# Cosine phases by an integer quarter turn on GpSimd, logs stacked on 64 rows, and another order of the round list

## The chip, the cores and the metric

The kernel runs on one core of a Trainium2 chip, in one launch. A core has five engines with queues of their own: TensorE (PE in the profile, with its weight loads as PEld), VectorE (DVE), ScalarE (ACT), GpSimd (POOL) and SyncE (SP, which only issues DMAs here). Each works its own queue in order and waits for semaphores. The metric is the device time in microseconds.

## The reference, cut to what matters

The block has two halves with a layer norm ahead of each, modulated by six vectors that a small product makes from `c`. The first half is a state space model (S4): a convolution along the 2048 positions, separately for each of 640 channels, with a kernel that is a sum over 128 complex exponentials.

```python
logdA = dt * (A_re + 1j * A_im)              # 640 x 128
dB = dt * (B_re + 1j * B_im)
P = jnp.exp(logdA[:, :, None] * l[None, None, :])      # l = 0 .. 2047
K = jnp.einsum("dn,dnl,dn->dl", Cc, P, dB).real        # 640 x 2048
y = irfft(rfft(u) * rfft(K)) + u * Dskip               # padded to 4096
x = x + ga * y
```

The second half is a gated product: `x + gb * ((silu(h w1) * (h w3)) w2)` with 640 x 1728 weights. The change touches the first half only.

## The kernel before, in words

The 2048 positions are split in 32 times 64. The exponential of the complex log at position 64 a + b is written as a magnitude times a cosine or sine of a phase, in a slow table (over a, 32 entries) and two fast ones (over b). The kernel K is then a small product over the 128 states, and both the convolution's transforms are products with constant matrices.

**Preparation.** `polar` (L237) takes the parameters of a slice of channels and makes magnitude logs and phases: the log of the magnitude per position (`are * dtc`), the log of the factor C times B, and the phases as integers, where 2^32 is a whole turn (`thi` for the turn per position, `phi` for the starting phase). It runs for channels 0 to 127 first with VectorE doing most products (`polar(d0, V)`), and for the other 512 in three stages in the loop over the first steps, with GpSimd in VectorE's place at some lines. Its last stage writes each log into `lt` in another order of columns, has TensorE transpose it into PSUM (L283), and splits it into a rounded part (`lah`, `lmh`, a copy on ScalarE) and the remainder (`lal`, `lml`, a subtraction on VectorE). TensorE's fast float mode keeps too few digits of one operand for a log; the two parts together have them.

**Steps.** The 640 channels are worked in 40 steps (`NS`) of 16 channels (`SD`). The names of the parts of a step s, as they stand in the round list:

- `PH`: `phases`, on GpSimd. L472 multiplies `thi` by the integers of `iota` (128x1024 integers, which wrap around at a turn) and L473 adds `phi` to the first 32 columns of each channel (128x512). The tile `ph` has four buffers.
- `AB`: `absph`, `CO`: `cosine`, `SI`: `sine`, all on ScalarE. The absolute value of the phase goes to the tile `cs` (three buffers), and the cosine is the sine of a quarter turn less that value, with the bias tile `hp`. The sine is taken of the phase in place.
- `PA`, `XA`, `PQ`, `XQ`: TensorE multiplies the logs by position tables (`exp_fast`, L432; `exp_slow`, L444), each for two ranges of 32 of the 128 contraction rows, and for rounded part and remainder as instructions of their own. ScalarE takes the exponential out of PSUM into the table `A`. Both products of all steps use one PSUM buffer (tag B) in the rounds.
- `E1`, `E2`, `A1`, `A2`: `real1` (L497, 128x1024), `real2` (L500, 128x512), `imag1` (L504, 128x1024), `imag2` (L508, 128x512) on VectorE: magnitudes times cosines into `E` (two buffers), magnitudes times sines in place in `A`. All their operands lie in SBUF.
- `kg` (L521), `K` (L528, L529), `pt` (L539), `uk`: the small product on TensorE, its scaling on VectorE, a first transform on TensorE, and a copy on ScalarE.

Ten steps behind, the convolution works on pieces k: `st` (L570, TensorE), `kc` (a copy on ScalarE), `T` (L587, L588: two products on VectorE, one operand in PSUM), `Y` (L594, L595: a difference and a sum, one operand in PSUM), `iv` (L612, TensorE) and `zt` (a copy on ScalarE and the store by SyncE). The PSUM buffer of `st` is single up to piece 38, so that `st` of k + 1 waits for `Y` of k.

**Order.** Steps 0 to 9 go through a loop over `tk`, beside the layer norm and a first transform of its result, with the order within an engine left to the framework but for ScalarE, whose order is the program's. From step 10 on the order is written out by hand: `ROUND` (L826) is a list of words, each a part and an offset, played once for every four steps (`EB`), and every instruction keeps its place in the queue of its engine. A part that has been done, or that is out of range, is passed over. A last loop (L846) does what is left of the convolution. Then the gated product begins.

Of the kernel before, what the change touches and what calls it, by code (L numbers as in the profile page):

```python
# [9 lines left out]
F32 = mybir.dt.float32  # L10
F32R = mybir.dt.float32r
I32 = mybir.dt.int32
# [5 lines left out]
P = 128  # L18
L = 2048
D = 640  # L20
# [87 lines left out]
def tile_kernel(ctx: ExitStack, tc: tile.TileContext, a):  # L108
# [28 lines left out]
    def acopy(out, in_):  # L137
        return tc.keep_in_program_order(S.copy(out, in_))  # L138
# [17 lines left out]
    gaT = kp.tile([P, D // 4], F32, name="gaT")  # L156
    dz = kp.tile([P, D // 4], F32, name="dz")
    V.memset(dz, 0.0)
    hp = kp.tile([P, 1], F32, name="hp")
    V.memset(hp, math.pi / 2)  # L160
    sc = kp.tile([P, KD], F32, name="sc")
    cT = kp.tile([P, KD], F32, name="cT")
    uk = kp.tile([P, 3, NA, DC], F32, name="uk")
# [6 lines left out]
    once = lambda shape, dt, name: tp.tile(shape, dt, name=name, bufs=1)  # L170
    thi = once([P, D], I32, "thi")
    phi = once([P, D], I32, "phi")
    lah = once([P, KD, P], F32R, "lah")
    lal = once([P, KD, P], F32R, "lal")
    lmh = once([P, KD, P], F32R, "lmh")
    lml = once([P, KD, P], F32R, "lml")
    r2 = once([P, NA, NB], F32R, "r2")
    r1 = once([P, NA, NA], F32R, "r1")
    sel = once([P, NA], F32R, "sel")
# [15 lines left out]
    flat = [uk[:, i].rearrange("p f d -> p (f d)") for i in range(3)]  # L195
    prm = flat[0][:, :6 * D].rearrange("p (i d) -> p i d", i=6)
    ldt, dt, m0, t3, gr, gi = (flat[2][:, i * D:(i + 1) * D] for i in range(6))

    def w_load(w, c0):

# [36 lines left out]
    def polar(cs, E):  # L237

        are, aim, br, bi, cr, ci = (prm[:, i, cs] for i in range(6))
        ld, dtc, m, t, g_r, g_i = (v[:, cs] for v in (ldt, dt, m0, t3, gr, gi))  # L240
        k0, nk = cs.start // P, (cs.stop - cs.start) // P

        E.tensor_tensor(g_r, br, cr, op=OP.mult)
        E.tensor_tensor(m, bi, ci, op=OP.mult)
        E.tensor_tensor(g_r, g_r, m, op=OP.subtract)
        V.tensor_tensor(g_i, br, ci, op=OP.mult)
        V.tensor_tensor(t, bi, cr, op=OP.mult)
        V.tensor_tensor(g_i, g_i, t, op=OP.add)
# [24 lines left out]

        nat = lambda v: v.rearrange("n (k p r j) -> n k r p j", k=nk, p=4, r=4)
        rows = lambda v: v[:, :nk * P].rearrange("n (k r p j) -> n k r p j", k=nk, p=4, r=4)
        for k in range(nk):
            E.tensor_tensor(rows(lt[:, 0])[:, k], nat(are)[:, k], nat(dtc)[:, k], op=OP.mult)
        for k in range(nk):
            V.tensor_tensor(rows(lt[:, 1])[:, k], nat(q)[:, k], nat(ld)[:, k], op=OP.add)
        for i, (hi, lo) in enumerate(((lah, lal), (lmh, lml))):  # L280
            pT = psS.tile([P, 2, 512], F32, name="pT", tag="AB"[i], bufs=1)
            for k in range(nk):
                PE.transpose(pT[:, 0, k * P:(k + 1) * P], lt[:, i, k * P:(k + 1) * P], ident)  # L283
# [132 lines left out]
    ph, cs, AA, EC, PK, K1 = {}, {}, {}, {}, {}, {}  # L416

    def exp_rows(s):
        return s // SPC, slice((s % SPC) // 2 * 8, (s % SPC) // 2 * 8 + 8), [
            (rr, slice((2 * (s % 2) + rr) * 32, (2 * (s % 2) + rr) * 32 + 32)) for rr in range(2)]  # L420

    pA, pQ = {}, {}

    def exp_fast(steps):

        for s in steps:
            pA[s] = psS.tile([P, 2, 512], F32, name="pa", tag="AB"[s % 2] if not in_order[0] else "B", bufs=1)
        for w, st in ((lah, True), (lal, False)):
            for s in steps:
                ch, js, rows = exp_rows(s)  # L430
                for rr, r in rows:
                    keep(PE.matmul(pA[s][:, rr, :], w[r, ch, :], r2[r, js, :].rearrange("p j b -> p (j b)"),  # L432
                                   start=st, stop=not st, tile_position=(r.start, 0)))

    def exp_slow(steps):

        for s in steps:
            pQ[s] = psS.tile([P, 2, 512], F32, name="pq", tag="AB"[s % 2] if not in_order[0] else "B", bufs=1)
        for i, (w, rt) in enumerate(((lah, r1), (lal, r1), (lmh, None), (lml, None))):
            for s in steps:  # L440
                ch, js, rows = exp_rows(s)
                for rr, r in rows:
                    rv = bc(sel[r, js], 2, NA) if rt is None else rt[r, js, :]
                    keep(PE.matmul(pQ[s][:, rr, :256], w[r, ch, :], rv,  # L444
                                   start=(i == 0), stop=(i == 3), tile_position=(r.start, 0)))

    def fast(s):

# [25 lines left out]
        ph[s] = p  # L474

    def absph(s):
        c = tp.tile([P, SD, NPH], F32, name="cs", bufs=3)
        act(c, ph[s], AF.Abs)
        cs[s] = c

    def cosine(s):
        act(cs[s], cs[s], AF.Sin, scale=-2 * math.pi / TURN, bias=hp)

    def sine(s):
        sn = ph[s].bitcast(F32)
# [11 lines left out]
        keep(V.tensor_tensor(EC[s][:, :, 1:3, :], AA[s][:, :, 1:3, :], mid(cs[s]), op=OP.mult))  # L497

    def real2(s):
        keep(V.tensor_tensor(EC[s][:, :, 0, :], AA[s][:, :, 0, :], cs.pop(s)[:, :, 2 * NA - 1:NA - 1:-1], op=OP.mult))  # L500

    def imag1(s):
        A = AA[s]
# [1 line left out]

    def imag2(s):
        A = AA[s]
        keep(V.scalar_tensor_tensor(A[:, :, 0, :], ph.pop(s)[:, :, 2 * NA - 1:NA - 1:-1], -1.0, A[:, :, 0, :],  # L508
                                    op0=OP.mult, op1=OP.mult))

    def tables(s):
# [262 lines left out]
    for tk in range(LAG):  # L774
# [49 lines left out]


    ROUND = (  # L826
# [5 lines left out]
    ).split()  # L832
    in_order[0] = True
    for rnd in range(NS // EB):
        for word in ROUND:
            name, k = word[:2].rstrip("+-"), EB * rnd + int(word[len(word[:2].rstrip("+-")):])
            do(name, k)
            if name == "E1" and 24 <= k < 32 and k % 2 == 0:
                x_load((k - 24) // 2)

            if name == "kg" and 36 <= k < 40:
# [681 lines left out]
```

## Time and profile before

| | |
|---|---|
| time, median of three runs | 984.4 us (982.26 to 985.58) |
| span of the profiled execution | 984.1 us, 20582 instructions |
| busy over the span: TensorE, VectorE, ScalarE, GpSimd | 918.2, 700.8, 541.1, 265.3 us |
| mean granted TensorE clock | 0.947 |
| HBM traffic | 142 GB/s over the span |

No time of the profiled execution other than its span is given, so sums are made against the span, which is 0.3 us under the median.

The span has four stretches: preparation (up to about 47 us), the loop over steps 0 to 9 (to about 173 us), the rounds and their end (to about 420 us), and the gated product. The shares over the whole span mix these; so the stages are read one by one, by the busy time of each engine in a window. A row of a group of instructions gives line, engine, operation, the tiles and their shapes and the count, then the busy time and the mean duration of one, then the idle time of the engine just before them and who ended it. A row in order of time begins with start and duration in us. Times of instructions that follow each other on one engine overlap by about a tenth of a microsecond, since the next begins while the last one drains.

### The profile page before, as it was taken

The numbers are of one execution on the slowest core, as the hardware profiler recorded it, in microseconds if no ns is written. First come the engines' busy times: TensorE is split into PE (matmuls) and PEld (weight loads), VectorE is DVE, ScalarE is ACT, GpSimd is POOL, SyncE is SP. The second block draws the span as 40 slices with busy tenths as digits, with TensorE's granted clock in tenths as the row PEclk, the third lists the DMA queues.
The fourth block names the chain that finished last, engine by engine and source line by source line (L and its number), as shares of the span: only waits on it lengthen the run. The fifth ranks groups of instructions, "written<-read, shape, count | busy, mean of one in ns | idle before, by whom it ended". The sixth has DMA issues, their size and how long they took to land.

```text
span 984.1 us, 20582 instructions
## 1 busy us (share of the span) xinstructions
PE 918.2 (93%) x8214; PEld 687.2 (70%) x8214; DVE 700.8 (71%) x1253; ACT 541.1 (55%) x793; POOL 265.3 (27%) x274
## 2 busy tenths in 40 slices
PE   5898797989888898789999999999999999999998
PEld 2445354766666676567888888777888888888886
DVE  4598856888988886667766665568796766654575
ACT  3667665899999983246433332355753333323432
POOL 1453333444444440214422220111152222200000
PEclk9855767999999999989999999999999999999999
DMA  9463576554665587767212311896432221113443
GB/s 267 159 228 110 220 186 186 158 131 134 159 159 154 153 219 200 252 170 259 82 55 62 99 54 52 221 281 208 135 93 67 81 68 54 54 41 90 151 148 120
DMA packets 103572, 140.74 MB, mean 143 GB/s; under 512 B 20565, under 2 KB 62677, under 8 KB 103477
## 3 DMA queue, kind: packets, MB, share of 16 engines
q1 hardware_dynamic: 99668, 129.34, 45.5%
q0 software_dynamic: 2304, 7.74, 2.4%
q10 hardware_dynamic: 1504, 2.36, 0.9%
q8 instruction: 64, 1.05, 0.4%
q14 instruction: 32, 0.25, 0.1%
HBM read 107.94 MB, written 31.46 MB: 142 GB/s over the span
## 4 chain that ended last, share of the span: by engine, by line
PE 68%; ACT 15%; DVE 7%; DMA 4%; issue 3%; POOL 2%; SPq 1%; ACTq 0%; DVEq 0%; POOLq 0%
PE ps L102 52%; ACT cs L135 4%; ACT A L135 3%; ACT ph L135 3%; PE pa L432 2%; PE p L570 2%; ACT L135 2%; DMA zs<-zt 2%; PE pq L444 2%; PE pt L539 1%; PE pk L521 1%; PE pm L299 1%; DMA A<-zs 1%; PE pu L406 1%; PE pz L612 1%
## 5 line engine op out<-in xcount | busy, mean ns | idle before, releaser
L102 DVE TENSOR_TENSOR s<-ps,s 128x512 f32<-128x512 f32 x138 | 94.8, 687 | 79.8 <-PE ps L102 79.5
L472 POOL TENSOR_TENSOR ph<-thi,iota 128x1024 int32<-128x1024 int32 x40 | 85.4, 2135 | 175.1 <-DVE A L508 78.2
L102 DVE TENSOR_TENSOR gl<-rw,gh 128x640 fp32r<-128x640 f32 x87 | 78.1, 897 | 65.3 <-ACT gh L102 65.2
L102 ACT CAST gh<-rw 128x640 fp32r<-128x640 f32 x87 | 63.3, 727 | 103.9 <-PE ps L102 60.6
L570 PE MATMUL p<-uk,s 128*64 128x256 f32 x640 | 79.0, 389 | 13.3 <-PE pa L432 5.6
L102 PE MATMUL ps<-xA,gh 128*128 128x512 f32 x280 | 87.9, 392 | 0.4 <-ACT xA L102 0.4
L102 PE MATMUL ps<-gh,uh 128*128 128x512 f32 x224 | 87.5, 390 | 0.0
L102 PE MATMUL ps<-gl,uh 128*128 128x512 f32 x224 | 87.2, 389 | 0.0
L102 POOL TENSOR_TENSOR S<-rw 128x256 f32<-128x256 f32 x46 | 36.7, 799 | 174.0 <-DVE S0l L102 163.1
L102 PE MATMUL ps<-gh,ul 128*128 128x512 f32 x208 | 81.1, 390 | 0.0
L570 PEld LDWEIGHTS p<-uk,s 128*64 128x64 f32 x640 | 45.2, 138 | 38.5 <-PE pa L432 8.4
L102 PEld LDWEIGHTS ps<-xA,gh 128*128 128x128 f32 x280 | 52.1, 188 | 13.0 <-ACT xA L102 1.0
L102 PE MATMUL ps<-xA,gl 128*128 128x512 f32 x140 | 54.5, 390 | 0.0
L135 ACT ACTIVATE A<-pa 128x1024 f32<-128x1024 f32 x40 | 40.4, 1023 | 25.7 <-PE pa L432 24.3
L497 DVE TENSOR_TENSOR E<-A,cs 128x1024 f32<-128x1024 f32 x40 | 51.0, 1275 | 1.7 <-PE pk L521 1.7
L504 DVE TENSOR_TENSOR A<-A,ph 128x1024 f32<-128x1024 f32 x40 | 50.1, 1253 | 0.0
L612 PE MATMUL pz<-Y,i 64*128 64x128 f32 x640 | 45.2, 286 | 5.0 <-issue 3.1
L612 PEld LDWEIGHTS pz<-Y,i 64*128 64x128 f32 x640 | 39.1, 190 | 14.9 <-issue 11.4
L102 PEld LDWEIGHTS ps<-gl,uh 128*128 128x128 f32 x224 | 42.1, 188 | 8.9
L102 PEld LDWEIGHTS ps<-gh,uh 128*128 128x128 f32 x224 | 42.0, 188 | 8.8
L521 PE MATMUL pk<-E 128*32 128x64 f32 x1280 | 46.6, 232 | 1.2 <-DVE E L500 0.6
L539 PE MATMUL pt<-s,K 128*64 128x128 f32 x640 | 47.2, 291 | 0.5 <-ACT uk L138 0.5
(261 smaller groups left out, 2306.7 us busy)
## 6 DMA issues: line engine op xcount, KB each, us to landing
rw<-in_w_dram SPq DMA_DIRECT2D x52, 320.0 KB
us<-u SPq DMA_DIRECT2D x16, 640.0 KB
s<-in_s_dram SPq DMA_DIRECT2D x40, 256.0 KB
i<-in_i_dram SPq DMA_DIRECT2D x40, 256.0 KB
rw<-in_wg_dram SPq DMA_DIRECT2D x31, 320.0 KB
rw<-in_wu_dram SPq DMA_DIRECT2D x28, 320.0 KB
uk<-us SPq DMA_DIRECT2D x32, 256.0 KB
zs<-zt SPq DMA_DIRECT2D x32, 256.0 KB
```

The source lines that it names most:

```text
L102: ins = fn(*args, **kw)
L135: return tc.keep_in_program_order(S.activation(*args, **kw))
L299: PE.matmul(pm[g, :n], scb[:, k], w[:, k, :], start=(k < 4), stop=(k > 0), tile_position=(0, g.start))
L432: keep(PE.matmul(pA[s][:, rr, :], w[r, ch, :], r2[r, js, :].rearrange("p j b -> p (j b)"), start=st, stop=not st, tile_position=(r.start, 0)))
L444: keep(PE.matmul(pQ[s][:, rr, :256], w[r, ch, :], rv, start=(i == 0), stop=(i == 3), tile_position=(r.start, 0)))
L472: hold(G.tensor_tensor(p, bc(thi[:, sl], 2, NPH), bc(iota, 1, SD), op=OP.mult))
L497: keep(V.tensor_tensor(EC[s][:, :, 1:3, :], AA[s][:, :, 1:3, :], mid(cs[s]), op=OP.mult))
L504: keep(V.tensor_tensor(A[:, :, 1:3, :], A[:, :, 1:3, :], mid(ph[s]), op=OP.mult))
L521: keep(PE.matmul(pk[dq * 32:dq * 32 + 32, g, :], x[:, g * 4 + dq, 1, :], x[:, g * 4 + dq, 0:3:2, :], start=(st == 0), stop=(st == 1), tile ...
L539: keep(PE.matmul(pt[c * 64:c * 64 + 64, g, :], kk[:, g, :], s1[:, c, :], start=True, stop=True, tile_position=(0, c * 64)))
L570: keep(PE.matmul(p2[par * 64:par * 64 + 64, pi, c, :], s2[:, pi * 2 + par, c * 64:c * 64 + 64], uk[:, 0:kn + 1:kn, f, :], start=True, stop ...
L612: ins = keep(PE.matmul(pz[:, par, (g % 2) * 2 + pi, :], i1[r, pi, c, :], Y[r, pi, c, :], start=(c == 0), stop=(c == 1), tile_position=(par ...
```

## The change

It has three parts.

1. **Quarter turn.** `absph` no longer takes an absolute value on ScalarE. It adds 2^30, a quarter turn, to the integer phase, on GpSimd, with the constant tile `quarter` broadcast over all columns; the addition wraps. The cosine is then the plain sine of that tile, without a bias tile. `AB` thus moves to GpSimd's queue.
2. **Stacked logs.** Rounded part and remainder of each log lie on 64 adjacent contraction rows (32 and 32) of one tile, `la` or `lm`, against a position table that repeats every 32 rows. One product over 64 rows replaces two over 32: two instead of four for `PA`, four instead of eight for `PQ`. In `polar` the split now comes ahead of the transposes: ScalarE rounds from SBUF into the scratch `l2`, VectorE subtracts into it, TensorE transposes twice as many blocks, and ScalarE copies the whole from PSUM. `l2` lies in the room of `gr` and `gi` and is used for one log after the other.
3. **Order.** The round list is written anew and shifted against the steps, runs for three more rounds (words without work are passed over, and a piece of the convolution beyond 41 is left to the last loop), and the last loop begins at 36.

```diff
-    hp = kp.tile([P, 1], F32, name="hp")
-    V.memset(hp, math.pi / 2)
+    quarter = kp.tile([P, 1], I32, name="quarter")
+    G.memset(quarter, 1 << 30)
...
-    lah = once([P, KD, P], F32R, "lah")
-    lal = once([P, KD, P], F32R, "lal")
-    lmh = once([P, KD, P], F32R, "lmh")
-    lml = once([P, KD, P], F32R, "lml")
+    la = once([P, 2 * KD, P], F32R, "la")
+    lm = once([P, 2 * KD, P], F32R, "lm")
...
+    l2 = flat[2][:, 4 * D:4 * D + 2 * (D - DC)]
...
-        for i, (hi, lo) in enumerate(((lah, lal), (lmh, lml))):
-            pT = psS.tile([P, 2, 512], F32, name="pT", tag="AB"[i], bufs=1)
-            for k in range(nk):
-                PE.transpose(pT[:, 0, k * P:(k + 1) * P], lt[:, i, k * P:(k + 1) * P], ident)
-            pv = pT[:, 0, :nk * P].rearrange("p (k n) -> p k n", k=nk)
-            acopy(hi[:, k0:k0 + nk], pv)
-            V.tensor_tensor(lo[:, k0:k0 + nk], pv, hi[:, k0:k0 + nk].bitcast(F32), op=OP.subtract)
+        for i, dst in enumerate((la, lm)):
+            raw = lt[:, i, :nk * P].rearrange("n (b c) -> n b c", c=32)
+            both = l2[:, :2 * nk * P].rearrange("n (b s c) -> n b s c", s=2, c=32)
+            acopy(both.bitcast(F32R)[:, :, 0], raw)
+            V.tensor_tensor(both[:, :, 1], raw, both[:, :, 0], op=OP.subtract)
+            pT = psS.tile([P, 2, 512], F32, name="pT", tag="AB"[i], bufs=1).rearrange("p a b -> p (a b)")
+            for k in range(nt):
+                PE.transpose(pT[:, k * P:(k + 1) * P], l2[:, k * P:(k + 1) * P], ident)
+            acopy(dst[:, 2 * k0:2 * k0 + nt], pT[:, :nt * P].rearrange("p (k n) -> p k n", k=nt))
...
     def exp_rows(s):
-        return s // SPC, slice((s % SPC) // 2 * 8, (s % SPC) // 2 * 8 + 8), [
-            (rr, slice((2 * (s % 2) + rr) * 32, (2 * (s % 2) + rr) * 32 + 32)) for rr in range(2)]
+        return s // 4, slice(s % 4 * 8, s % 4 * 8 + 8), [(rr, slice(rr * 64, rr * 64 + 64)) for rr in range(2)]
...
-        for w, st in ((lah, True), (lal, False)):
-            for s in steps:
-                ch, js, rows = exp_rows(s)
-                for rr, r in rows:
-                    keep(PE.matmul(pA[s][:, rr, :], w[r, ch, :], r2[r, js, :].rearrange("p j b -> p (j b)"),
-                                   start=st, stop=not st, tile_position=(r.start, 0)))
+            t, js, rows = exp_rows(s)
+            for rr, r in rows:
+                keep(PE.matmul(pA[s][:, rr, :], la[r, t, :], r2[r, js, :].rearrange("p j b -> p (j b)"),
+                               start=True, stop=True, tile_position=(r.start, 0)))
...
     def absph(s):
-        c = tp.tile([P, SD, NPH], F32, name="cs", bufs=3)
-        act(c, ph[s], AF.Abs)
+        c = tp.tile([P, SD, NPH], I32, name="cs", bufs=3)
+        keep(G.tensor_tensor(c, ph[s], bc(quarter, 1, SD).broadcast_to([P, SD, NPH]), op=OP.add))
         cs[s] = c

     def cosine(s):
-        act(cs[s], cs[s], AF.Sin, scale=-2 * math.pi / TURN, bias=hp)
+        c = cs[s].bitcast(F32)
+        act(c, cs[s], AF.Sin, scale=2 * math.pi / TURN)
+        cs[s] = c
...
     ROUND = (
-        "E1+2 kc+2 pt+0 CO+4 PH+5 T+2 kg+1 SI+3 PA+4 K+1 SI+4 Y+2 uk+0 E2+2 st+3 E1+3 XA+4 A1+2 kc+3 "
-        "PQ+4 A2+2 pt+1 XQ+4 T+3 PH+6 PA+5 kg+2 XA+5 Y+3 uk+1 K+2 PQ+5 st+4 A1+3 XQ+5 zt+1 E1+4 AB+5 "
-        "PA+6 E2+3 pt+2 XA+6 A2+3 E2+4 kc+4 PQ+6 uk+2 PH+7 T+4 kg+3 XQ+6 AB+6 PA+7 K+3 iv+2 XA+7 AB+7 "
-        "Y+4 PQ+7 A1+4 st+5 XQ+7 A2+4 PH+8 kg+4 CO+5 iv+3 kc+5 K+4 CO+6 T+5 pt+3 zt+3 Y+5 uk+3 E1+5 "
-        "SI+5 st+6 CO+7 E2+5 A1+5 SI+6 iv+4 AB+8 A2+5 iv+5 "
+        "uk+0 K+1 st+3 PQ+4 kc+3 XQ+4 pt+1 A2+2 PA+5 E1+3 kg+2 T+3 XA+5 uk+1 PQ+5 XQ+5 zt+1 Y+3 PA+6 XA+6 "
+        "E1+4 st+4 PQ+6 K+2 E2+3 A1+3 A2+3 iv+2 XQ+6 PA+7 pt+2 E2+4 kc+4 XA+7 T+4 PQ+7 PH+6 kg+3 Y+4 AB+6 "
+        "uk+2 XQ+7 A1+4 st+5 CO+5 kc+5 A2+4 K+3 PH+7 E1+5 iv+3 AB+7 pt+3 SI+5 PH+8 CO+6 uk+3 T+5 E2+5 zt+3 "
+        "kg+4 Y+5 SI+7 K+4 st+6 CO+7 SI+6 E1+6 A1+5 E2+6 AB+8 pt+4 kc+6 CO+8 PA+8 SI+8 A2+5 XA+8 iv+4 T+6 "
+        "PH+9 AB+9 kg+5 Y+6 iv+5 A1+6 "
     ).split()
     in_order[0] = True
-    for rnd in range(NS // EB):
+    for rnd in range(NS // EB + 3):
         for word in ROUND:
             name, k = word[:2].rstrip("+-"), EB * rnd + int(word[len(word[:2].rstrip("+-")):])
+            if all((n, NS - 1) in done for n in parts) or (name in conv and k > NS + 1):
+                continue
...
-    for tk in range(NS + 1, LAG + 8 * NDC + 2):
+    for tk in range(NS - 4, LAG + 8 * NDC + 2):
```

More of the change, by code (lines that the diff above doesn't have):

```diff
@@ L272, in polar @@
         yield
-        nat = lambda v: v.rearrange("n (k p r j) -> n k r p j", k=nk, p=4, r=4)
-        rows = lambda v: v[:, :nk * P].rearrange("n (k r p j) -> n k r p j", k=nk, p=4, r=4)
-        for k in range(nk):
+        nt = 2 * nk
+        nat = lambda v: v.rearrange("n (t p r j) -> n t r p j", t=nt, p=4, r=2)
+        rows = lambda v: v[:, :nk * P].rearrange("n (t r p j) -> n t r p j", t=nt, p=4, r=2)
+        for k in range(nt):
             E.tensor_tensor(rows(lt[:, 0])[:, k], nat(are)[:, k], nat(dtc)[:, k], op=OP.mult)
-        for k in range(nk):
+        for k in range(nt):
             V.tensor_tensor(rows(lt[:, 1])[:, k], nat(q)[:, k], nat(ld)[:, k], op=OP.add)
-        for i, (hi, lo) in enumerate(((lah, lal), (lmh, lml))):
-            pT = psS.tile([P, 2, 512], F32, name="pT", tag="AB"[i], bufs=1)
-            for k in range(nk):
-                PE.transpose(pT[:, 0, k * P:(k + 1) * P], lt[:, i, k * P:(k + 1) * P], ident)
-            pv = pT[:, 0, :nk * P].rearrange("p (k n) -> p k n", k=nk)
-            acopy(hi[:, k0:k0 + nk], pv)
-            V.tensor_tensor(lo[:, k0:k0 + nk], pv, hi[:, k0:k0 + nk].bitcast(F32), op=OP.subtract)
+        for i, dst in enumerate((la, lm)):
[4 more added lines that the diff above has]
+            pT = psS.tile([P, 2, 512], F32, name="pT", tag="AB"[i], bufs=1).rearrange("p a b -> p (a b)")
+            for k in range(nt):
+                PE.transpose(pT[:, k * P:(k + 1) * P], l2[:, k * P:(k + 1) * P], ident)
+            acopy(dst[:, 2 * k0:2 * k0 + nt], pT[:, :nt * P].rearrange("p (k n) -> p k n", k=nt))
         V.tensor_scalar(m, m, 0.5 / math.pi, 0.125, op0=OP.mult, op1=OP.add)
@@ L438, in exp_slow @@
             pQ[s] = psS.tile([P, 2, 512], F32, name="pq", tag="AB"[s % 2] if not in_order[0] else "B", bufs=1)
-        for i, (w, rt) in enumerate(((lah, r1), (lal, r1), (lmh, None), (lml, None))):
-            for s in steps:
-                ch, js, rows = exp_rows(s)
+            t, js, rows = exp_rows(s)
+            for i, w in enumerate((la, lm)):
                 for rr, r in rows:
-                    rv = bc(sel[r, js], 2, NA) if rt is None else rt[r, js, :]
-                    keep(PE.matmul(pQ[s][:, rr, :256], w[r, ch, :], rv,
-                                   start=(i == 0), stop=(i == 3), tile_position=(r.start, 0)))
+                    keep(PE.matmul(pQ[s][:, rr, :256], w[r, t, :], bc(sel[r, js], 2, NA) if i else r1[r, js, :],
+                                   start=(i == 0), stop=(i == 1), tile_position=(r.start, 0)))
     def fast(s):
@@ L499, in real2 @@
     def real2(s):
-        keep(V.tensor_tensor(EC[s][:, :, 0, :], AA[s][:, :, 0, :], cs.pop(s)[:, :, 2 * NA - 1:NA - 1:-1], op=OP.mult))
+        keep(V.tensor_tensor(EC[s][:, :, 0, :], AA[s][:, :, 0, :], cs[s][:, :, 2 * NA - 1:NA - 1:-1], op=OP.mult))
     def imag1(s):
@@ L507, in imag2 @@
         A = AA[s]
-        keep(V.scalar_tensor_tensor(A[:, :, 0, :], ph.pop(s)[:, :, 2 * NA - 1:NA - 1:-1], -1.0, A[:, :, 0, :],
+        keep(V.scalar_tensor_tensor(A[:, :, 0, :], ph[s][:, :, 2 * NA - 1:NA - 1:-1], -1.0, A[:, :, 0, :],
                                     op0=OP.mult, op1=OP.mult))
@@ L839, in tile_kernel @@
                 x_load((k - 24) // 2)
-            if name == "kg" and 36 <= k < 40:
+            if name == "kg" and 36 <= k < NS:
                 early.append((None, z_tile()))
```

## The prediction

> **What bounds the kernel now.** I read the busy times by stage first, then the groups of one stretch of whole rounds, then the order of time on GpSimd and VectorE. By stage (columns: window, then busy us and instructions of each engine, granted clock):
>
> ```profile
> core 0: us, PE busy (x) PEld busy (x) DVE busy (x) ACT busy (x) POOL busy (x), PEclk, DMA share, GB/s
> 47.00:173.00 126.00, 106.55 (x1314) 59.05 (x1316) 98.18 (x170) 85.11 (x102) 48.15 (x39) 0.66 0.59 185
> 173.00:347.32 174.32, 157.76 (x3078) 115.92 (x3078) 150.94 (x249) 159.52 (x195) 82.54 (x53) 1.00 0.57 150
> ...
> 262.25:290.61 28.36, 25.65 (x500) 18.73 (x500) 24.50 (x41) 26.34 (x32) 12.97 (x8) 1.00 0.61 158
> ```
>
> Up to 173 us the steps 0 to 9 run at a granted clock of 0.66 and no engine is full. From 173 us the list of rounds runs; a round of four steps lasts 28.36 us, and ScalarE is busy for 26.34 of them. From 400 us on stands the gated product, which the change does not touch. The change can act on about 350 us, and most of it in the rounds. Their groups, over five rounds (205.54 to 347.32; busy us and mean ns, then idle time before):
>
> ```profile
> L472 POOL TENSOR_TENSOR ph<-thi,iota 128x1024 int32<-128x1024 int32 x20 | 43.9, 2196 | 74.0 <-DVE A L508 54.0 <-ACT A L135 20.1
> L504 DVE TENSOR_TENSOR A<-A,ph 128x1024 f32<-128x1024 f32 x21 | 25.5, 1215 | 0.0
> L497 DVE TENSOR_TENSOR E<-A,cs 128x1024 f32<-128x1024 f32 x20 | 24.3, 1217 | 0.0
> L135 ACT ACTIVATE cs<-cs,hp 128x1024 f32<-128x1024 f32 x20 | 23.1, 1155 | 0.1
> ...
> L135 ACT ACTIVATE cs<-ph 128x1024 f32<-128x1024 int32 x20 | 21.3, 1064 | 0.0
> L473 POOL TENSOR_TENSOR ph<-ph,phi 128x512 int32<-128x512 int32 x20 | 20.9, 1046 | 1.6
> L135 ACT ACTIVATE ph<-ph 128x1024 f32<-128x1024 int32 x20 | 20.7, 1064 | 0.0
> L135 ACT ACTIVATE A<-pa 128x1024 f32<-128x1024 f32 x20 | 20.5, 1024 | 6.4 <-PE pa L432 5.4
> ...
> L508 DVE SCALAR_TENSOR_TENSOR A<-ph,A 128x512 f32<-128x512 f32 x20 | 13.7, 684 | 0.2
> L500 DVE TENSOR_TENSOR E<-A,cs 128x512 f32<-128x512 f32 x20 | 13.7, 683 | 0.0
> ...
> L135 ACT ACT_TABLE_LOAD x10 | 12.8, 1283 | 0.2
> L135 ACT ACTIVATE A<-pq 128x512 f32<-128x512 f32 x20 | 12.1, 604 | 3.4 <-PE pq L444 3.4
> ```
>
> ScalarE waits only for the two exponent products: 6.4 + 3.4 us in five rounds, 2.0 a round, which with 26.34 makes the round. So ScalarE bounds it, by busy time. The absolute values cost it 21.3 / 5 = 4.26 us a round: what the change takes away is on the path. Whether the gain stays depends on where that work goes.
>
> **GpSimd and VectorE exclude each other.** That is the row which decides. Late in the first steps, GpSimd (first four) and VectorE (last four) in order of time (start, duration):
>
> ```profile
> 148.79 2.82 POOL L472 TENSOR_TENSOR ph<-thi,iota 128x1024 int32<-128x1024 int32 x1 [6.59 <-DVE pk L528]
> 151.69 1.37 POOL L473 TENSOR_TENSOR ph<-ph,phi 128x512 int32<-128x512 int32 x1
> 155.36 1.90 POOL L472 TENSOR_TENSOR ph<-thi,iota 128x1024 int32<-128x1024 int32 x1 [2.29 <-DVE pk L528]
> 157.34 1.91 POOL L473 TENSOR_TENSOR ph<-ph,phi 128x512 int32<-128x512 int32 x1
> ...
> 148.64 1.21 DVE L497 TENSOR_TENSOR E<-A,cs 128x1024 f32<-128x1024 f32 x1
> 150.10 2.06 DVE L500 TENSOR_TENSOR E<-A,cs 128x512 f32<-128x512 f32 x1
> 152.08 2.06 DVE L504 TENSOR_TENSOR A<-A,ph 128x1024 f32<-128x1024 f32 x1
> 155.73 2.60 DVE L497 TENSOR_TENSOR E<-A,cs 128x1024 f32<-128x1024 f32 x1
> ```
>
> Follow the ends. L497 ends at 149.85; L472, issued before that, ends 1.76 us later (151.61). L500 was issued at 150.10 and ends 0.55 after L472 (152.16). L473 then ends 0.90 later (153.06), L504 another 1.08 later (154.14). They take turns, and the loser waits for a whole instruction: L500 took 2.06 us instead of 0.68, L497 2.60 instead of 1.22. In the rounds it is different for the products that read PSUM:
>
> ```profile
> 279.53 1.22 DVE L497 TENSOR_TENSOR E<-A,cs 128x1024 f32<-128x1024 f32 x1
> 279.76 2.76 POOL L472 TENSOR_TENSOR ph<-thi,iota 128x1024 int32<-128x1024 int32 x1 [4.62 <-DVE A L508]
> ...
> 287.21 1.90 POOL L472 TENSOR_TENSOR ph<-thi,iota 128x1024 int32<-128x1024 int32 x1 [3.57 <-DVE A L508]
> 287.70 0.70 DVE L588 TENSOR_TENSOR p<-p,kc 128x512 f32<-128x512 f32 x1
> ```
>
> The first L472 waits for L497 to end (280.75, less some 0.1) and then takes its 1.9 us; the second runs beside L588, which has one operand in PSUM, and neither is slowed. So the four VectorE products of a step with both operands in SBUF (L497, L500, L504, L508) and GpSimd's phase work share one resource; I call it the port. Time on it per step: GpSimd 1.76 + 0.90 = 2.66, VectorE 1.08 + 0.55 + 1.08 + 0.55 = 3.26; a round of before needs 4 x 5.92 = 23.7 of its 28.36 us. It fits, because the old list lets each phase start after A2, when T and Y, which read PSUM, come next.
>
> **The change part by part.**
>
> *Absolute value off ScalarE.* ScalarE loses 4.26 us a round, and the cosine, now from integers without a bias tile, costs 1064 instead of 1155 ns (as the sine's row), 0.36 a round: 26.34 falls to 21.7. Nothing of this can be lost unless another resource lasts longer.
>
> *The quarter turn on GpSimd.* One integer addition of 128x1024 for each step. No row shows it. From below, 0.90 on the port if it cost no more than the 512 elements of L473; from above 2.76, the longest L472 with its wait. I take 1.80: twice L473, which is the same addition of a tile and a broadcast operand, and close to L472's 1.76 for the same 1024 elements. Port time per step becomes 2.66 + 1.80 + 3.26 = 7.72, so a round cannot be under 30.9 us while all of it excludes.
>
> The trace cannot show that this new form excludes. The Trainium skill, "SBUF — State Buffer", section "Who interferes with whom", says that a VectorE instruction with two SBUF inputs contends with any GpSimd instruction that reads SBUF, that the one which starts first keeps the pair for its whole length, and that one with at most one SBUF input does not contend. By that rule the addition counts in full and the sum is the 30.9 above; the rows agree with it in both halves. "GPSIMD Engine Reference" of the same skill, section "3.1 Elementwise — side-by-side cycle accounting", gives 4497 ns for an addition of 2048 elements; an estimate from it is 2.25 us for ours, a round of 32.7 at least. L472's 1.90 for 1024 elements is measured here, and stays.
>
> *The new order, walked by hand with these times*, from the end of A2+5 (0.0), VectorE's others by their pitch (T 1.4, Y 0.75, K 0.55). PH+9 runs beside T+6 and Y+6 and holds A1+6 back to 3.0-4.1; AB+9 to 5.9 holds back A2+2 (to 6.5); E1+3 to 7.6; PH+6 to 10.4, holding E1+4 (to 11.5); nobody has the port during K+2, since AB+6 waits for E2+3 to free a cosine buffer (12.65); A1+3 13.75; AB+6 15.55; A2+3 and E2+4 16.7; PH+7 19.5; A1+4 20.6; AB+7 22.4; A2+4 23.0; half of PH+8 25.0; E1+5 26.1; the other half 27.0; free until E2+5 (28.1); AB+8 30.0; E1+6 31.1; A1+5 32.2; E2+6 32.8; A2+5 33.4. So 33.4 us a round: 30.9, 1.1 of free port, 1.4 of handing over. ScalarE and TensorE keep up: CO+8 behind AB+8 is free at 30.1 and its cosine is wanted by E1+4 of the next round, some 14 us later. The lock-limited part goes from AB of step 12 to that of step 39, 27 steps or 6.75 rounds: 6.75 x (33.4 - 28.36) = **+34.0 us**, with 30.9 as the lower end (+17).
>
> *Logs on 64 rows.* Half of the exponent products go:
>
> ```profile
> 264.06 0.50 PE L432 MATMUL pa<-r,lah 32*128 32x512 f32 x2
> 264.40 0.40 PE L432 MATMUL pa<-r,lal 32*128 32x512 f32 x2
> ...
> 266.14 0.28 PE L444 MATMUL pq<-r,lal 32*128 32x256 f32 x2
> 266.25 0.27 PE L444 MATMUL pq<-sel,lmh 32*128 32x256 f32 x2
> ```
>
> By the starts a pair costs 0.34 (264.06 to 264.40) and 0.11 (266.14 to 266.25): 0.34 + 2 x 0.11 = 0.56 a step, 2.2 of TensorE's 25.65 a round. In port-bound rounds this is worth nothing. In the first steps TensorE is at 106.55 of 126 us: eight steps there, at clock 0.66, give 8 x 0.56 / 0.66 = 6.8 us if all on the path, and ScalarE's lost absolute values 12 x 1.15 = 13.8, at most; with no engine full I take 4 together (between 0 and 14).
>
> *The quarter turn in the first steps.* VectorE's port products are 10 x 3.26 of those 126 us, 26%. Twelve additions of 1.8 hit them for 12 x 1.8 x 0.26 = 5.6; I take **+5**, between 0 and 21.6 (every one in VectorE's way).
>
> *The logs' split.* It now precedes the transposes, through one scratch tile, so the second log's copy waits for the first's transposes. For steps 0 to 7 ScalarE has room behind it:
>
> ```profile
> 25.34 1.02 ACT L135 ACTIVATE A<-pa 128x1024 f32<-128x1024 f32 x1 [9.19 <-PE pa L432]
> ...
> 105.88 1.11 PE L283 MATMUL pT<-ident,lt 128*128 128x128 f32 x4
> ...
> L138 ACT COPY zt<-pz 128x1024 f32<-128x1024 f32 x10 | 10.0, 1002 | 0.0
> ```
>
> 9.19 us of waiting before the first exponential hide the added copy and addition (if that cover went, some 1 us). For the other 32 steps there are eight more transposes (2 x 1.11) and two more copies of 1.00, which delay the x tiles behind them on ScalarE: 4.2 if nothing hides, 0 if all is hidden; I take **+2**. GpSimd's products there become eight of half the size. The moved memset is free.
>
> *Ends of the list.* The last convolution steps now partly run in the loop behind the rounds, in the order they had; no instruction is added, and GpSimd's loads of z keep their place behind the last phases. Zero, ±2.
>
> Sum: 984.1 (the profiled span; no other time of that execution is shown, and the runs' median is 984.4, so nothing is added) + 34 - 4 + 5 + 2 = **1021**.
>
> **The rivals.**
> - *The port does not bind.* Then VectorE is next with 24.5 us a round; walking the list without the port, T+4 waits 0.8 for its copy and E1+5 0.7 for the cosine behind the table load: 26.3. 6.75 x (28.36 - 26.3) = -14, -4 and +2 outside: 968. It decides once the addition holds the port under (28.36 - 23.7) / 4 = 1.17 us. For it: the additions may be quicker than L473 says; against: four turns in a row above.
> - *GpSimd late, cosines exposed.* CO+8 stands right behind AB+8 on ScalarE, and ahead of a table load and the next exponentials. If each step shows 1.06 of cosine between its addition and its product, a round is 33.4 + 4.2 = 37.6: 984.1 + 62 + 3 = 1049. Against: three cosine buffers, and the walk leaves 14 us.
> - *Nothing comes of it:* the addition holds the port about 1.2 us, the round stays near 28.4, the rest cancels: 984.
>
> **How the numbers follow.** Port-bound rounds 0.73, its own range 1001 (30.9 a round) to 1042 (2.25 us an addition and every early addition in the way); late cosines 0.09; port not binding 0.15; nothing 0.03. Runs of this kernel spread over 0.3%, so about 3 us is no change. Faster 0.15, same 0.03, slower 0.82. From 990 to 1045 about 0.8 lies inside; left out are the faster rival and the top of the late one.
>
> **What would show it.** In the rounds: a period of 31 to 35 us; ScalarE near 21.7 busy a round with real idle time; the addition at 1.9 when alone and 2.5 to 3 on average; L497, L500, L504 with means well over 1.22 and 0.68, and GpSimd and VectorE both looking nearly full. A period under 28 with those means unchanged proves me wrong: then the addition is short or does not exclude. A period over 36 with ScalarE idle ahead of cosines is the late rival.

## The result and the profile after

The changed kernel takes 1023.8 us (median of four runs, 1022.9 to 1026.9) against 985.0 us before: a ratio of 1.040, with a 95% interval of 1.0372 to 1.0428. It is slower by 39 us. The profiled execution has a span of 1025.1 us against 984.1, 41.0 more.

Busy time by stage after the change (same columns as before; the first window is that of the first steps, the second and third are two rounds, cut where GpSimd begins the phase of the same step):

```profile
core 0: us, PE busy (x) PEld busy (x) DVE busy (x) ACT busy (x) POOL busy (x), PEclk, DMA share, GB/s
47.00:173.00 126.00, 99.35 (x1152) 53.78 (x1150) 109.02 (x167) 68.63 (x85) 70.41 (x55) 0.63 0.57 176
...
267.14:300.70 33.56, 24.94 (x460) 18.04 (x462) 33.04 (x41) 21.00 (x27) 24.64 (x13) 0.92 0.45 124
300.70:334.26 33.56, 26.44 (x486) 19.63 (x484) 33.04 (x41) 23.05 (x30) 24.64 (x13) 0.93 0.48 127
```

A round lasts 33.56 us instead of 28.36. ScalarE has fallen from 26.34 busy microseconds to about 22 and is idle for a third of the round. VectorE looks full, 33.04 of 33.56, though it has the same instructions as before, which took 24.50. The groups say which of them grew (four rounds, 233.58 to 367.82):

```profile
L475 POOL TENSOR_TENSOR cs<-ph,quarter 128x1024 int32<-128x1024 int32 x16 | 38.4, 2402 | 14.8 <-DVE E L499 14.2
L496 DVE TENSOR_TENSOR E<-A,cs 128x1024 f32<-128x1024 f32 x16 | 38.1, 2384 | 0.0
L469 POOL TENSOR_TENSOR ph<-thi,iota 128x1024 int32<-128x1024 int32 x17 | 37.8, 2223 | 20.3 <-DVE A L507 16.8 <-DVE pk L527 3.5
L507 DVE SCALAR_TENSOR_TENSOR A<-ph,A 128x512 f32<-128x512 f32 x16 | 25.7, 1608 | 0.0
L470 POOL TENSOR_TENSOR ph<-ph,phi 128x512 int32<-128x512 int32 x16 | 24.4, 1525 | 1.3
L503 DVE TENSOR_TENSOR A<-A,ph 128x1024 f32<-128x1024 f32 x16 | 22.0, 1377 | 0.0
...
L135 ACT ACTIVATE cs<-cs 128x1024 f32<-128x1024 int32 x16 | 16.9, 1055 | 0.0
...
L587 DVE TENSOR_TENSOR p<-p,kc 128x512 f32<-128x512 f32 x16 | 11.2, 700 | 0.6
L499 DVE TENSOR_TENSOR E<-A,cs 128x512 f32<-128x512 f32 x16 | 10.9, 680 | 0.0
```

L496 is the old L497, L499 the old L500, L503 the old L504 and L507 the old L508. Three of the four products with both operands in SBUF are longer: 2384 against 1217 ns, 1608 against 684, 1377 against 1215. Together that is 2.25 us a step, 9.0 a round. The fourth (L499, E2) has stayed at 680. The product with an operand in PSUM (L587, before L588) has stayed at 700 ns. In order of time, GpSimd (first four) and VectorE:

```profile
267.14 1.91 POOL L469 TENSOR_TENSOR ph<-thi,iota 128x1024 int32<-128x1024 int32 x1 [0.70 <-DVE pk L527]
269.12 1.90 POOL L470 TENSOR_TENSOR ph<-ph,phi 128x512 int32<-128x512 int32 x1
272.22 1.89 POOL L475 TENSOR_TENSOR cs<-ph,quarter 128x1024 int32<-128x1024 int32 x1 [1.19 <-DVE E L499]
...
290.40 2.74 POOL L475 TENSOR_TENSOR cs<-ph,quarter 128x1024 int32<-128x1024 int32 x1 [2.36 <-DVE E L499]
...
267.45 2.67 DVE L496 TENSOR_TENSOR E<-A,cs 128x1024 f32<-128x1024 f32 x1
270.05 0.68 DVE L586 TENSOR_TENSOR T<-p,kc 128x512 f32<-128x512 f32 x1
...
272.30 0.41 DVE L594 TENSOR_TENSOR Y<-T,p 128x256 f32<-128x256 f32 x1
...
273.17 2.03 DVE L496 TENSOR_TENSOR E<-A,cs 128x1024 f32<-128x1024 f32 x1
...
290.17 1.22 DVE L503 TENSOR_TENSOR A<-A,ph 128x1024 f32<-128x1024 f32 x1
291.31 2.38 DVE L507 SCALAR_TENSOR_TENSOR A<-ph,A 128x512 f32<-128x512 f32 x1
```

The first L496 begins 0.3 us after L469, waits until that ends (269.05) and ends 1.07 us later (270.12); L470, issued in between, waits for it and ends 0.90 later (271.02). L475, the new addition, does the same to the next L496: it ends at 274.11, and L496 at 275.20, again 1.09 later. Y (L594, one operand in PSUM) runs beside it in its usual 0.41 us, and K (L528, one operand in PSUM) at 272.82 in its usual 0.42. Later it goes the other way as well: the addition issued at 290.40, released by E2, waits for A1 (L503), which ends at 291.39; it ends 1.75 us after that (293.14), and A2 (L507), issued in between, ends 0.55 later (293.69). The chain of work inside a round is now VectorE alone (its first line for 267.14 to 300.70):

```profile
by line: DVE E L496 27.5%; DVE A L507 18.5%; DVE A L503 12.3%; DVE p L587 8.4%; DVE T L586 7.3%; DVE K L528 6.3%; issue 6.2%; DVE E L499 5.5%; DVE Y L594 4.2%; DVE Y L593 3.9%; DVE pk L527 1.1%; DVEq L593 0.1%
```

### The profile page after: what moved, and what is told of

The parts are those of the page before. It is cut to its first block, busy times and chain, and to the rows that moved or that the text cites. A ratio compares the mean times of both kernels' runs of the same rounds, so it can differ in the third digit from the quotient of the medians.

```text
span 1025.1 us, 20184 instructions
## 1 busy us (share of the span) xinstructions
PE 917.8 (90%) x7984; PEld 687.1 (67%) x7984; DVE 772.0 (75%) x1258; ACT 505.2 (49%) x757; POOL 369.8 (36%) x319
## 4 chain that ended last, share of the span: by engine, by line
PE 60%; DVE 29%; ACT 3%; issue 3%; DMA 2%; POOL 2%; ACTq 0%; DVEq 0%; SPq 0%; POOLq 0%
PE ps L102 51%; DVE E L496 6%; DVE A L507 5%; DVE A L503 4%; DVE E L499 2%; DVE p L587 2%; DVE T L586 2%; DMA zs<-zt 2%; DVE K L528 1%; PE pu L408 1%; PE p L569 1%; PE pm L301 1%; DVE Y L594 1%; DVE Y L593 1%; PE pt L538 1%
## 5 line engine op out<-in xcount | busy, mean ns | idle before, releaser
L569 PE MATMUL p<-uk,s 128*64 128x256 f32 x640 | 88.8, 425 | 34.8 <-issue 18.6
L469 POOL TENSOR_TENSOR ph<-thi,iota 128x1024 int32<-128x1024 int32 x40 | 86.3, 2159 | 70.8 <-DVE A L507 38.1
L475 POOL TENSOR_TENSOR cs<-ph,quarter 128x1024 int32<-128x1024 int32 x40 | 91.8, 2294 | 51.3 <-DVE E L499 46.5
L496 DVE TENSOR_TENSOR E<-A,cs 128x1024 f32<-128x1024 f32 x40 | 77.9, 1949 | 1.2 <-ACT A L135 0.8
L503 DVE TENSOR_TENSOR A<-A,ph 128x1024 f32<-128x1024 f32 x40 | 59.8, 1495 | 0.0
L138 ACT COPY kc<-p 128x512 f32<-128x512 f32 x40 | 23.4, 585 | 72.9 <-issue 36.6
L507 DVE SCALAR_TENSOR_TENSOR A<-ph,A 128x512 f32<-128x512 f32 x40 | 57.8, 1446 | 0.0
L538 PE MATMUL pt<-s,K 128*64 128x128 f32 x640 | 51.1, 305 | 6.9 <-DVE K L528 6.9
L470 POOL TENSOR_TENSOR ph<-ph,phi 128x512 int32<-128x512 int32 x40 | 55.7, 1393 | 3.8 <-DVE phi L293 1.0
L538 PEld LDWEIGHTS pt<-s,K 128*64 128x64 f32 x640 | 41.9, 154 | 15.2 <-ACT cs L135 7.3
L520 PE MATMUL pk<-A 128*32 128x64 f32 x1280 | 46.1, 234 | 6.4 <-DVE A L507 6.4
```

The source lines that it names most:

```text
L469: hold(G.tensor_tensor(p, bc(thi[:, sl], 2, NPH), bc(iota, 1, SD), op=OP.mult))
L470: keep(G.tensor_tensor(p[:, :, :NA], p[:, :, :NA], bc(phi[:, sl], 2, NA), op=OP.add))
L475: keep(G.tensor_tensor(c, ph[s], bc(quarter, 1, SD).broadcast_to([P, SD, NPH]), op=OP.add))
L503: keep(V.tensor_tensor(A[:, :, 1:3, :], A[:, :, 1:3, :], mid(ph[s]), op=OP.mult))
L507: keep(V.scalar_tensor_tensor(A[:, :, 0, :], ph[s][:, :, 2 * NA - 1:NA - 1:-1], -1.0, A[:, :, 0, :], op0=OP.mult, op1=OP.mult))
L520: keep(PE.matmul(pk[dq * 32:dq * 32 + 32, g, :], x[:, g * 4 + dq, 1, :], x[:, g * 4 + dq, 0:3:2, :], start=(st == 0), stop=(st == 1), tile ...
```

## The experiments

My theory was that GpSimd's addition and VectorE's products of two SBUF operands exclude each other, so that a round must hold both, one after the other. The rivals: that the new list is to blame; that the logs' split costs what is lost before the rounds; and that the addition is only late in GpSimd's queue, whatever it touches. The table gives all kernels with marks read from their profiles: the start of the first VectorE product (E1) of step 9; the length of a round, as a third of the time from E1 of step 17 to that of step 29; and the time from E1 of step 39 to the start of the last T. Each mark is from one execution; up to step 11 e1, e6, e7 and e8 run the same instructions, and their marks for step 9 lie between 145.6 and 149.8, so that a few us there mean nothing. The before-kernel ran at 984.8 us (median) beside e1 to e4 and at 986.3 beside e5 to e8.

| kernel | time, us | ratio to before (95%) | step 9 | round | end |
|---|---|---|---|---|---|
| before | 985.0 | | 148.6 | 28.35 | 44.3 |
| changed | 1023.8 | 1.040 (1.0372 to 1.0428) | 161.1 | 33.56 | 40.1 |
| e1: changed, absolute value back | 980.0 | 0.9936 (0.9912 to 0.9960) | 146.1 | 28.23 | 40.0 |
| e2: before, quarter turn | 1036.5 | 1.0506 (1.0467 to 1.0545) | 158.9 | 34.83 | 42.7 |
| e3: before, stacked logs | 985.3 | 1.0024 (0.9997 to 1.0051) | 149.5 | 28.54 | 43.8 |
| e4: before, new list | 992.1 | 1.0075 (1.0049 to 1.0101) | 149.9 | 29.71 | 39.4 |
| e5: changed, GpSimd only writes | 974.0 | 0.9880 (0.9841 to 0.9918) | 145.8 | 27.92 | 41.5 |
| e6: changed, quarter turn from step 12 | 1012.2 | 1.0278 (1.0241 to 1.0316) | 146.3 | 33.56 | 40.5 |
| e7: changed, quarter turn in one step of four | 988.4 | 1.0021 (1.0001 to 1.0041) | 145.6 | 29.41 | 39.6 |
| e8: changed, in two steps of four | 998.4 | 1.0124 (1.0093 to 1.0154) | 149.8 | 31.13 | 41.5 |

### e1: the absolute value back on ScalarE

```diff
-        c = tp.tile([P, SD, NPH], I32, name="cs", bufs=3)
-        keep(G.tensor_tensor(c, ph[s], bc(quarter, 1, SD).broadcast_to([P, SD, NPH]), op=OP.add))
+        c = tp.tile([P, SD, NPH], F32, name="cs", bufs=3)
+        act(c, ph[s], AF.Abs)
...
-        act(c, cs[s], AF.Sin, scale=2 * math.pi / TURN)
+        act(cs[s], cs[s], AF.Sin, scale=-2 * math.pi / TURN, bias=hp)
```

> The changed kernel with the absolute value and the biased cosine back on ScalarE; stacked logs and the new round list stay. Port theory (GpSimd's addition and VectorE's products of two SBUF operands exclude each other): a round needs 23.7 us of port and 26.3 of ScalarE, so the period falls from 33.6 to 27 to 28.5 us, L496 and L499 go back to 1.22 and 0.68 us, and the time is 970 to 990 us. Order theory (the new list makes the rounds long): the period stays over 31 us and the time over 1005.

980.0 us, and a round of 28.23. The stage row and the groups between 240 and 340 us:

```profile
241.91:270.15 28.24, 24.87 (x476) 18.68 (x472) 25.47 (x41) 26.25 (x33) 13.86 (x9) 0.94 0.58 151
...
L494 DVE TENSOR_TENSOR E<-A,cs 128x1024 f32<-128x1024 f32 x14 | 20.3, 1449 | 2.9 <-ACT cs L135 2.9
...
L505 DVE SCALAR_TENSOR_TENSOR A<-ph,A 128x512 f32<-128x512 f32 x15 | 10.2, 682 | 0.0
L497 DVE TENSOR_TENSOR E<-A,cs 128x512 f32<-128x512 f32 x14 | 9.6, 684 | 0.0
```

ScalarE is full again at 26.25, A2 is back at 682 ns. E1 is not quite back: 1449 ns, not 1220, since the new list starts some phases right ahead of it. The two other parts of the change make the kernel a little faster, so in this list the 44 us between 980.0 and 1023.8 are all the quarter turn's. This is the fastest kernel of the study with all of the computation, 0.6% ahead of the kernel before.

### e2: the quarter turn alone, in the old list

The edits of `absph`, `cosine` and the constant tile, and nothing else, in the kernel before.

> The kernel before with the quarter turn on GpSimd alone; old logs, old round list. Port theory: not under 30.9 us a round whatever the order, 31 to 36 us in this list, which puts no PSUM product beside the addition; 1005 to 1045 us. Order theory: the old list hides the addition, ScalarE falls to 21.7 us, a period of 25 to 28.4, at most 985 us.

1036.5 us, a round of 34.83. So the old list does not hide the addition either; the order theory falls, from both sides, for e4 shows what the list alone does. Groups between 240 and 340 us:

```profile
L478 POOL TENSOR_TENSOR cs<-ph,quarter 128x1024 int32<-128x1024 int32 x12 | 28.1, 2349 | 11.0 <-DVE E L502 11.0
...
L506 DVE TENSOR_TENSOR A<-A,ph 128x1024 f32<-128x1024 f32 x12 | 20.1, 1674 | 0.0
L510 DVE SCALAR_TENSOR_TENSOR A<-ph,A 128x512 f32<-128x512 f32 x12 | 16.7, 1390 | 0.1
```

Here it is A1 (1674 ns) and A2 (1390) that are held up: the addition waits for E2 to free a cosine tile, and starts as A1 and A2 are due.

### e3: the stacked logs alone

The edits of `polar`, `exp_rows`, `exp_fast` and `exp_slow` in the kernel before.

> The kernel before with the stacked logs alone. Both theories: TensorE 2.2 us a round shorter, ScalarE's waits for the exponent products fall from 2.0 to about 1.2 us, period 27.3 to 28.2 us; in the first steps the split costs 0 to 5 us and the fewer products give 0 to 7. 968 to 984 us. If the split is what costs the 12 us that the changed kernel loses up to step 9, this one shows them.

985.3 us, no change that can be measured, and a round of 28.54: a miss on both counts, for I expected 968 to 984 us and 27.3 to 28.2. The split does not cost the loss before the rounds: step 9 comes at 149.5. TensorE is faster and nothing comes of it, because other waits of ScalarE take the place (240 to 340 us):

```profile
L501 DVE TENSOR_TENSOR A<-A,ph 128x1024 f32<-128x1024 f32 x14 | 18.6, 1328 | 0.0
...
L135 ACT ACTIVATE cs<-ph 128x1024 f32<-128x1024 int32 x15 | 16.0, 1070 | 3.2 <-POOL ph L470 3.2
...
L135 ACT ACTIVATE A<-pa 128x1024 f32<-128x1024 f32 x13 | 13.4, 1030 | 3.0 <-PE pa L431 2.9
...
L135 ACT ACTIVATE A<-pq 128x512 f32<-128x512 f32 x13 | 7.8, 602 | 0.6
```

The wait for the second exponent product is down from 2.0 in the same window of the kernel before to 0.6, but ScalarE now waits 3.2 us for phases that are late on GpSimd, and A1 has grown to 1328 ns. In order of time the end of a phase now reaches into an A1: L470 ends at 263.46, and the A1 issued at 263.24 takes 1.31 us. Why the phases start later was not followed further.

### e4: the new list alone

The round list and its loops in the kernel before, the absolute value as a ScalarE instruction at the places of `AB`.

> The kernel before with the new round list alone, the absolute value being ScalarE's. Port theory: ScalarE bounds it as before, 28 to 29.5 us a round, no product of VectorE slowed by more than 10 per cent on average, 980 to 995 us. Order theory: over 31 us a round, over 1005 us.

992.1 us, slower by 0.75%, a round of 29.71: 1.36 more than before, a quarter of what the changed kernel loses in a round. That is just over the 29.5 that I had set as the upper end; the time is within its range. The products are not longer (L497 at 1221 ns). ScalarE waits more for the exponents (240 to 340 us; 3.9 and 2.0 before), VectorE for the cosine (6.1) and, ahead of T, for the copy `kc` (10.4, not in the lines below):

```profile
L497 DVE TENSOR_TENSOR E<-A,cs 128x1024 f32<-128x1024 f32 x13 | 15.9, 1221 | 6.5 <-ACT cs L135 6.1
...
L135 ACT ACTIVATE A<-pa 128x1024 f32<-128x1024 f32 x14 | 14.3, 1024 | 5.3 <-PE pa L432 5.3
...
L135 ACT ACTIVATE A<-pq 128x512 f32<-128x512 f32 x14 | 8.5, 606 | 7.1 <-PE pq L444 7.1
```

With the shorter exponent products (e1) the same list gives 28.23. List and logs belong together: alone they cost 7 us and nothing, together they gain 5. The end of the list is another matter: it lasts 39.4 to 41.5 us in the seven kernels with the new list, and 42.7 to 44.3 in the three with the old one.

### e5: GpSimd only writes

```diff
-        keep(G.tensor_tensor(c, ph[s], bc(quarter, 1, SD).broadcast_to([P, SD, NPH]), op=OP.add))
+        for _ in range(2):
+            keep(G.memset(c, 1 << 30))
```

> The changed kernel with two memsets of the whole cosine tile on GpSimd in place of its addition: by the 0.53 us of the 512-element memset behind the rounds, about 2.1 us, as long as the addition, but it reads nothing from SBUF. What is left out: the cosines, whose tile holds a constant; everything behind them runs as before. Port theory (what excludes is two readers of SBUF): a round has 23.7 us of port, VectorE's 24.5 us of work bound it, period 26 to 28 us, L496 under 1.5 us on average, time 960 to 985. Rival, GpSimd's time or its place in the queue (the addition is late, whatever it touches): GpSimd stays as busy as it was, period 31 to 34 us, time over 1005.

974.0 us and a round of 27.92. GpSimd is about as busy with the two memsets (1.96 us a pair) as with an unhindered addition (1.9). In order of time:

```profile
259.33 1.96 POOL L476 MEMSET cs<- 128x1024 int32 x2 [2.28 <-DVE E L500]
261.26 2.11 POOL L469 TENSOR_TENSOR ph<-thi,iota 128x1024 int32<-128x1024 int32 x1
...
259.19 1.22 DVE L504 TENSOR_TENSOR A<-A,ph 128x1024 f32<-128x1024 f32 x1
260.32 0.68 DVE L508 SCALAR_TENSOR_TENSOR A<-ph,A 128x512 f32<-128x512 f32 x1
260.93 0.68 DVE L500 TENSOR_TENSOR E<-A,cs 128x512 f32<-128x512 f32 x1
```

Three products of two SBUF operands run through the two memsets without a delay on either side. The memsets no longer wait for the phase, which is a second difference to the addition. But step 9 comes at 145.8 and the rounds are short with GpSimd busier than in the changed kernel (78.6 against 73.3 us between 240 and 340) and the memsets at the same places in its queue, waiting for E2 as the addition does. So neither GpSimd's time nor its queue is the cause. The memset writes the same tile and reads nothing: what excludes is the reading. One expectation was missed: E1 (L497 in this kernel) takes 1710 ns on average, not under 1500, since phases still start ahead of it.

### e6: the quarter turn only from step 12 on

```diff
-        keep(G.tensor_tensor(c, ph[s], bc(quarter, 1, SD).broadcast_to([P, SD, NPH]), op=OP.add))
+        if s >= 12:
+            keep(G.tensor_tensor(c, ph[s], bc(quarter, 1, SD).broadcast_to([P, SD, NPH]), op=OP.add))
+        else:
+            act(c.bitcast(F32), ph[s], AF.Abs)
```

(The kernel has the condition as a small function; `cosine` follows it likewise.)

> The changed kernel with the quarter turn only from step 12 on, the absolute value on ScalarE for steps 0 to 11. Undone: what the addition costs before the rounds. The changed kernel's step 9 comes 14.9 us later than in the kernel with the absolute value back, so this should start the rounds 13 to 16 us earlier, with a period of 33.6 us as it was: 1006 to 1013 us. Rival, that the loss before the rounds is one of arrangement and comes back in them: 1018 to 1025.

1012.2 us, with the round at 33.56 to the hundredth as in the changed kernel. So the twelve early additions cost 11.6 us, and the loss there does not come back later. Over steps 0 to 11 the four VectorE products take 63.6 us in all in the changed kernel and 51.0 in e1. The whole difference is in A1 and A2 (36.1 against 23.2); E1 and E2 are unchanged (27.5 against 27.7). Two places in the changed kernel (GpSimd, then VectorE):

```profile
89.61 1.94 POOL L475 TENSOR_TENSOR cs<-ph,quarter 128x1024 int32<-128x1024 int32 x1 [7.42 <-DVE E L499]
...
99.60 1.90 POOL L475 TENSOR_TENSOR cs<-ph,quarter 128x1024 int32<-128x1024 int32 x1
...
89.71 2.92 DVE L503 TENSOR_TENSOR A<-A,ph 128x1024 f32<-128x1024 f32 x1
...
99.67 1.84 DVE L383 SCALAR_TENSOR_TENSOR rs<-mv,rs 128x2 f32<-128x2 f32 x1 [0.86 <-POOL rs L382]
```

The first addition was released by E2 and takes the port just ahead of A1, which lasts 2.92 instead of 1.22. The second takes it 0.07 us ahead of a layer norm's scale: 128x2 numbers, which take 0.16 us when nothing holds them, take 1.84. This happens to two of the eight scales (to one of eight in e1 and before, behind a phase). ScalarE waits for these scales; between 47 and 173 us, in the changed kernel and in e1 (us in total, times, longest):

```profile
ACT x L135 <- DVE rs L383: 17.2, 5, 7.3
```

```profile
ACT x L135 <- DVE rs L383: 6.9, 5, 3.3
```

The two held scales explain some 3 us of this difference at most: the longest wait, 7.3, ends at 82.42 behind a scale that took its usual 0.16, so most of it is VectorE being late as a whole. With the memsets (e5) the same wait is 10.5 us and step 9 is not late, so this row alone does not measure the loss.

### e7 and e8: one and two steps of four

The changed kernel with the condition `s >= 12 and s % 4 == 1` (e7) or `s >= 12 and s % 2 == 1` (e8) in place of e6's `s >= 12`.

> Stacked logs and the new list, the quarter turn on GpSimd only for steps 13, 17, 21 and so on (the addition that the list puts behind PH+9). Port sum 23.7 + 1.8 = 25.5 us a round, ScalarE 26.3 - 1.2 = 25.2: if only sums count, a period of 27.0 to 28.2 and 970 to 981 us, at or under the 980.0 of the kernel with the absolute value back. If every addition costs its full turn on VectorE, 28.2 + 1.3 = 29.5 us a round, about 989.

> The same for every odd step from 13 on: port sum 23.7 + 3.6 = 27.3 us a round. Port theory with the handing over seen in the changed kernel (33.6 against 30.9, a factor of 1.09): 29 to 30.5 us a round, 985 to 998 us. If ScalarE's relief counts in full (24.0 us): under 28.2, under 980.

988.4 and 998.4 us; rounds of 29.41 and 31.13. With 28.23 for none (e1) and 33.56 for four, an addition costs 1.18, 1.45 and 1.33 us of a round (1.18 / 1, 2.90 / 2, 5.33 / 4). e7 came out as the second of its two cases, the full turn; e8 lies just above its range, in the period (29 to 30.5) and in the time (985 to 998). For e7 the sums alone would have allowed a gain; instead each addition costs from the first one on. The groups of e7 between 240 and 340 us:

```profile
L505 DVE TENSOR_TENSOR E<-A,cs 128x1024 f32<-128x1024 f32 x14 | 26.7, 1905 | 0.0
...
L479 POOL TENSOR_TENSOR cs<-ph,quarter 128x1024 int32<-128x1024 int32 x3 | 7.7, 2577 | 0.2
```

One addition in four steps lifts the mean of E1 from 1449 to 1905 ns. In this list VectorE had hardly any time left: e5, which takes the absolute value off ScalarE and asks nothing of the port for it, is only 0.3 us a round shorter than e1, with VectorE busy for 97.8 of the 100 us from 240 to 340. So even where ScalarE's 4.6 us a round are on the path, the next limit, VectorE with the phases' share of the port, lies close behind.

## Why the prediction was right, point by point

- **ScalarE bounds the kernel, and loses 4.6 us a round.** The loss is right: 26.34 fell to between 21.0 and 23.1 (forecast 21.7), the cosine to 1055 ns (1064 forecast). That ScalarE bounded the old rounds was read from 26.34 of 28.36 us and not tested apart. e5 shows what its relief is worth in the new list when the addition does not read: 0.3 us a round against e1.
- **GpSimd's addition excludes VectorE's products of two SBUF operands, and T, Y and K do not take part.** Right, shown from four sides: the ends in the trace, e1 (taken away), e5 (kept busy without reading), e7 and e8 (in doses). The addition lasts 1.89 us alone and held the port for 1.75 from the end of A1 (291.39 to 293.14); I took 1.80. The 2.25 us that I had estimated from the Trainium skill, "GPSIMD Engine Reference", section "3.1 Elementwise — side-by-side cycle accounting", would have been too long. The Trainium skill, "SBUF — State Buffer", section "Who interferes with whom", says that a VectorE instruction with two SBUF inputs contends with a GpSimd instruction that reads SBUF, and not with one that only writes it. e5 agrees with the second half: three products took their usual 1.22, 0.68 and 0.68 us beside the memsets.
- **A round of 33.4 us.** 33.56. The round of 33.4 worked out by hand, less VectorE's 24.5 us of work, has it held back by about 9 us; the groups show 9.0. The bare sum of port times, 30.9, would have been 2.7 short. By the records, in each of the two rounds shown one of the two engines has a port instruction open for 32.1 of the 33.56 us, and neither has for the other 1.5; the forecast had 1.1 of free port and 1.4 of handing over.
- **+34 us in the rounds.** From E1 of step 9 to that of step 39 the changed kernel needs 252.5 us against 220.5 before (413.59 - 161.05 and 369.16 - 148.64): +32.0. By the runs, e6 against e1, 32.1. On the stretch that the prediction priced, from AB of step 12 to that of step 39, it is 232.1 against 196.5 us: +35.5 for a forecast of +34.0.
- **+3 us before the rounds: wrong size.** Measured +12.4 at step 9, or +7.7 at AB of step 12: the changed kernel is quicker through steps 9 to 12, so where the rounds are said to begin decides a few us. The term that failed is "12 x 1.8 x 0.26 = 5.6" for the additions in the first steps. It let them fall anywhere in VectorE's time. They do not: about half of these additions wait for E2 to free the tile, and so start when A1 or A2 is due; these two products alone take 12.8 us more than in e1 over the twelve steps. Two of the layer norms' scales, which I had not counted among the port's users, are held up as well. Measured: 11.6 us. The gain of 4 from the shorter products and from ScalarE and the cost of 2 from the split cannot be told apart: with the absolute value back (e1, e6, e7, e8) step 9 comes between 145.6 and 149.8, against 148.6 and 149.9 in the two kernels that have the old preparation and the absolute value.
- **Ends of the list: zero, within 2.** Wrong: from E1 of step 39 to the last T the changed kernel needs 40.1 us instead of 44.3, which gives 4.2 back. It goes with the new list (e4 alone has it, e3 has not); which word does it was not looked into.
- Sum of the three: 12.4 + 32.0 - 4.2 = 40.2 of the 41.0 between the spans. 1021 against 1023.8 was thus right in its main term, and two smaller errors, +9 and -4, stood against each other; that they did so is luck.
- **The rivals.** That the port does not bind was ruled out by e1 and e5; its price was wrong as well: e5 gives 27.92 us a round, not 26.3, and E1 takes 1710 ns there: the walk without the port left out that the phases still hold it. Late cosines: ScalarE's waits in the rounds are for copies and exponents; the groups of four rounds have 0.0 idle ahead of the cosine, and 0.0 on VectorE ahead of E1.
- **The signs and the bounds.** Period, ScalarE's idle time, the addition's 1.9 alone and the longer E1 and A1 came as named. Not so: E2 (L499), which was to grow, stayed at 680 ns while A2 grew instead; the addition's mean is 2402 ns, just under "2.5 to 3"; and GpSimd is busy for 24.64 of 33.56 us, not nearly full. The range given for the port-bound case alone does not follow from its terms: 30.9 us a round with the other terms gives about 1004, not 1001, and 2.25 us an addition (35.2 us a round by the walk) with every early addition in the way about 1050, not 1042.

## What to carry to other kernels

Before work goes to GpSimd, add up the time in which its instructions read SBUF and the time of VectorE's instructions with two SBUF operands: for the instructions of this kernel the two were one resource, and a round that needed 30.9 us of it took 33.56 while GpSimd looked idle for a quarter of it. A busy engine in the profile may be a waiting one; the mean of a group against its shortest instance in the whole run tells (L496: 1949 against 1166 ns). In the rounds alone it would not, since there even the shortest is held (1928). And an instruction that is released by one product of a series starts as the next one is due: the collision can then be the rule, as it was here, and a share of the time is no estimate for it.

## What I had not expected of the hardware

An instruction on two numbers per partition (L383, 0.16 us) waits for a whole GpSimd addition, 1.84 us, as a large one does: it has two SBUF operands, as the large ones have, and its size made no difference. And GpSimd's memsets of 128x1024 numbers (0.95 us each, 1.96 for two) run beside VectorE's products at no cost to either (e5).
